# A denominator tile with a step of its own, larger packets, and a new order of issue in an attention and gated MLP kernel

## The chip, the cores and the metric

The kernel runs on one core of a Trainium2 chip. The metric is the device time of one execution in microseconds; lower is better. Engines are named as in the profile: PE (TensorE, matmuls), DVE (VectorE), ACT (ScalarE), POOL (GpSimd), SP (SyncE, which here issues the DMAs).

## The reference

Eight batches of 12 heads, 448 positions, head size 64. Attention with a soft cap on the scores is followed by a feed-forward part whose second half is mixed over the positions.

```python
scores = scale * np.matmul(q, k.transpose(0, 1, 3, 2))
scores = cap * np.tanh(scores / cap)
scores = scores - np.max(scores, axis=-1, keepdims=True)
attn = np.exp(scores)
attn = attn / (np.sum(attn, axis=-1, keepdims=True) + 1e-09)
x = np.matmul(attn, v)            # heads side by side: B, S, 768
...
h = np.maximum(x @ w_in, 0.0)
u, v = (h[..., :d_ff // 2], h[..., d_ff // 2:])
v_n = (v - mu) / np.sqrt(var + 1e-06)
v_s = np.einsum('ts,bsd->btd', w_spatial, v_n) + b_spatial[None, :, None]
return ((u * v_s) @ w_out).astype(np.float32)
```

## The kernel before

Work is cut into 24 quads (four heads of one batch, three quads a batch) and eight feed-forward parts. A quad in `quad_bnd` loads two raw tiles of q and k (`raw`) and four tiles of v, and makes seven groups of scores on PE (`sc`, four 64x64 matmuls in fp32). Each group is followed by a tanh on ACT, every two of them by one exponential (the last group has one of its own), and by a PE group that multiplies the exponentials with v into `x` (`pv`). Scores have two buffers, so group n can start when tanh n-2 is done.

The denominators take a side way. DVE folds the exponentials to their maximum and sum (`red`, `st`). For the first three quads PE makes the sums, with a matrix of ones (`ones`), and they go through DRAM (`td`) into the small tile `dt`. ACT shifts rows of `st` into `sh`, DVE combines both in `dt` and takes the reciprocal, two DMAs write it to DRAM (`rd`), and two DMAs broadcast it over the partitions (`rr`). Then DVE multiplies it into the copied `x` (`xf`), ACT and DVE make a high and a low half of it (`xg`), and the feed-forward part can use it: large matmuls of 128 rows, called `moe` here.

No engine's order is written out. `Plan.order` simulates the engines with fixed costs, and takes at each time the ready task with the lowest key; keys come from tables (`BND_KEY`, `BND_ADJ`) of about 130 numbers. The chosen order is recorded, and each engine then runs its instructions in that order, each as soon as its semaphores allow. SP issues all DMAs, in one order too. A task with an `allocs` list claims a buffer when it is taken. On PE a change from the 64-row matmuls to the large ones, or back, adds `STICK` to a key. The first weights are split into high and low parts (`w`, `wy`, `wi_h`, `wi_l`) during the first quads, on POOL, DVE and ACT.

Quads are counted from 0, and groups of scores and tanhs from 1, over the whole run.

Of the kernel before, what the change touches and what calls it, by code (L numbers as in the profile page):

```python
# [42 lines left out]
class Plan:  # L43
# [165 lines left out]
def gpc(n):  # L209
# [29 lines left out]
BND_KEY = dict(ld=15.1316, vld=10.6595, sc=-4.3972, th=0.8221, ex=-13.3346, pv=2.8747, sm=5.6221, mx=2.7207,  # L239
               dn=-3.5316, ev=-2.5342, x=1.255, moe=3.3159, span=11.7552, step=-1.2625, mv=-7.4324, vld_=0.4935, sc_=0.475,  # L240
               th_=0.213, ex_=2.8729, pv_=0.0973, sm_=0.5533, mx_=0.887)
BND_ADJ = dict(sc0=1.8257, sc1=1.698, sc2=0.6056, sc3=3.487, sc4=2.4891, sc5=0.9848, sc6=1.9465, sc7=1.2566,
               sc8=-0.2027, sc9=-0.0525, sc10=-1.0199, sc11=-1.6861, sc21=0.372, sc22=0.2759, sc23=-0.0304, mx0=4.147, mx1=2.3102,
               mx2=-1.5569, mx3=-2.5816, mx4=-1.7021, mx5=-3.8682, mx6=-3.7708, mx7=-2.1194, mx8=2.2658, mx9=6.0412, mx10=4.2055,
               mx11=1.3621, mx21=-0.5191, mx22=-1.2175, mx23=5.0057, sm0=1.8357, sm1=-4.3389, sm2=0.1127, sm3=-1.9888,
               sm4=-3.2252, sm5=-6.4566, sm6=-4.1062, sm7=-2.4598, sm8=-0.1718, sm9=4.6664, sm10=2.3463, sm11=0.4051,
               sm21=-1.2777, sm22=-3.1044, sm23=2.1372, dn0=-6.9641, dn1=1.8515, dn2=-0.9662, dn3=3.7809, dn4=8.6087, dn5=5.0673,
               dn6=1.1656, dn7=-2.366, dn8=0.4341, dn9=2.5001, dn10=4.9471, dn11=-4.3505, dn21=14.2648, dn22=10.8391, dn23=8.4438,
               x0=-1.2869, x1=-4.0561, x2=-5.6099, x3=-5.4773, x4=2.351, x5=0.6484, x6=4.0904, x7=0.1021, x8=2.4533, x9=6.1666,
               x10=4.3613, x11=1.3018, x21=-0.0656, x22=-3.6008, x23=0.1225, moe0=-0.4749, moe1=-0.3715, moe2=-0.6357,  # L250
               moe3=-0.003, moe7=-4.8205, span0=0.237, span1=0.5291, span2=-5.1693, span3=-3.6031, span7=51.1417, mv0=3.2517,
               mv1=1.1849, mv2=5.0071, mv3=5.7847, mv7=-5.1134, wi0=-11.8899, wi1=-7.682, wi2=-25.3033, wi3=9.6125, wi4=12.6292,
               wi5=4.2564, wi6=0.1225, wi7=-1.8938, wi8=-6.6204, wi9=0.3494, wi10=-1.8774, wi11=-9.6153, ws0=-12.9749, ws1=4.598,
               ws2=-15.4035, ws3=-9.2649, wo0=-5.5216, wo1=-4.7934, wo2=-5.3784, wo3=1.0364)
# [12 lines left out]
def attn_moe(ctx, tc, bounded, shared, qk, v, qk2, v2, cap, w_in, w_sp, w_out, out):  # L267
# [183 lines left out]

    def head_any(b, h, vt, vdep, xf, rr, after):
# [102 lines left out]
    def quad_bnd(b, n):  # L555
# [5 lines left out]
        for c in range(2):  # L561
            hp = 2 * n + c
            t = Buf("xg" if b * NP + hp in SPARE else "raw")
            raw.append(t)
# [12 lines left out]
        for i in range(NB):
# [22 lines left out]
            def pv(g=i // 2, tp=tp):  # L600
                for j in range(2 if g < 3 else 1):
                    for c in range(2):
                        for e in range(2):
# [1 line left out]
                            nc.tensor.matmul(x.t[e * D:(e + 1) * D, c, :S], lhsT=vts[g].t[c * D:(c + 1) * D, (2 * j + e) * D:(2 * j + e + 1) * D],  # L605
                                             rhs=tp.t[c * D:(c + 1) * D, j * PW + e * S:j * PW + (e + 1) * S], start=(k == 0), stop=(k == NB - 1))

            prev = add("T", FF * w // PW, kk("pv", i), pv, [ex, prev, tvs[i // 2]], [vts[i // 2], tp, x], [x] if i == 1 else [], name="pv", mode="R")
# [32 lines left out]
        d = add("V", 106, kk("dn"), lambda: nc.vector.tensor_tensor(sec(0), st.t[:96, :n1], sh.t[:96, :n1], op=ALU.max), d,  # L641
                [st, sh, dt], [dt], name="mred2")
        if by_pe:
# [300 lines left out]
```

## Time and profile before

| what | value |
|---|---|
| median of 3 runs | 734.66 us (734.47 to 735.39) |
| the profiled execution's own time | 735.29 us |
| its span, first to last instruction | 733.5 us |
| granted TensorE clock, mean | 0.994 of 2.4 GHz |
| DMA, mean over the span | 91 GB/s |

The span is what the trace covers; 1.8 us of the profiled execution lie around it. Busy times are shares of the span by engine. PE's busy time holds pipelined matmuls with modelled ends, so that 98% busy does not say that PE works at its peak.

### The profile page before, as it was taken

To read this page: it belongs to the slowest core of one execution; us is meant where nothing else is said; L and a number is where in the kernel's file an instruction comes from. 1 tells how busy PE (TensorE), PEld (TensorE's weight loads), DVE (VectorE), ACT (ScalarE), POOL (GpSimd) and SP (SyncE) were. 2 spreads that over 40 slices of the span, in tenths; PEclk is the share of its full clock that TensorE was granted. 3 is DMA by queue.
4 is the path that set the end of the run, shared out by engine and by line. 5 is a ranking of instruction groups with operands and counts; after the bars stand their busy time and mean duration, and the time that the engine had idled before them with its cause. 6 is when DMAs were issued, how large, how long until landed. Compare 5 with 4: busy or idle time off the path is not lost.

```text
span 733.5 us, 12340 instructions
## 1 busy us (share of the span) xinstructions
PE 716.0 (98%) x4902; PEld 485.3 (66%) x4902; DVE 609.6 (83%) x825; ACT 481.4 (66%) x648; POOL 79.0 (11%) x69
## 2 busy tenths in 40 slices
PE   8997999999999999999999999999999999999997
PEld 2333675574587586955778557767659576679896
DVE  4999999999999998949999299989899598884620
ACT  6999865858856957388573794867773865833421
POOL 1353011500100002000210003000020001000100
PEclk9998999999999999999999999999999999999999
DMA  7556232533212432052230431214311321002002
GB/s 268 192 192 200 67 111 63 164 102 107 90 32 85 143 100 76 1 150 82 72 102 11 140 103 33 69 44 160 101 47 56 101 76 51 26 26 88 14 2 80
DMA packets 43167, 66.52 MB, mean 91 GB/s; under 512 B 8782, under 2 KB 33884, under 8 KB 43100
## 3 DMA queue, kind: packets, MB, share of 16 engines
q1 hardware_dynamic: 43100, 65.64, 28.3%
q8 instruction: 40, 0.66, 0.4%
q14 instruction: 27, 0.22, 0.1%
HBM read 54.42 MB, written 11.20 MB: 89 GB/s over the span
## 4 chain that ended last, share of the span: by engine, by line
PE 63%; DVE 21%; ACT 6%; DMA 5%; issue 3%; SPq 1%; POOL 0%; DVEq 0%; ACTq 0%
PE ps_s L584 10%; PE ps_x L605 9%; DVE red L623 8%; PE ps_acc L859 4%; PE ps_acc L860 4%; PE ps_acc L861 4%; PE ps_acc L743 4%; PE ps_acc L744 4%; PE ps_acc L745 4%; DMA rr<-rd 3%; PE ps_acc L768 2%; PE ps_acc L770 2%; PE ps_acc L769 2%; ACT tp L595 2%; PE ps_acc L837 2%
## 5 line engine op out<-in xcount | busy, mean ns | idle before, releaser
L588 ACT ACTIVATE tp<-ps_s,capt 128x896 f32<-128x896 f32 x168 | 162.3, 1005 | 19.7 <-PE ps_s L584 13.7
L595 ACT ACTIVATE tp<-tp,capt 128x1792 f32<-128x1792 f32 x96 | 154.3, 1609 | 1.5
L623 DVE TENSOR_TENSOR red<-red,tp 128x1792 f32<-128x1792 f32 x90 | 140.0, 1555 | 14.7 <-ACT tp L595 13.2
L584 PE MATMUL ps_s<-raw 64*64 64x448 f32 x1344 | 147.1, 544 | 3.0 <-ACT tp L588 2.7
L605 PE MATMUL ps_x<-tp,v 64*64 64x448 f32 x1344 | 140.6, 537 | 2.0 <-ACT tp L595 1.7
L623 DVE TENSOR_TENSOR red<-tp 128x1792 f32<-128x1792 f32 x45 | 90.9, 2021 | 24.1 <-ACT tp L595 23.1
L605 PEld LDWEIGHTS ps_x<-tp,v 64*64 64x64 f32 x1344 | 50.4, 133 | 78.2 <-issue 67.8
L584 PEld LDWEIGHTS ps_s<-raw 64*64 64x64 f32 x1344 | 46.2, 132 | 80.4 <-issue 43.8
L792 POOL TENSOR_TENSOR lst<-lst,capt 128x1 f32<-128x1 f32 x32 | 38.6, 1208 | 521.8 <-DVE lst L790 521.8
L743 PE MATMUL ps_acc<-xg,wi_h 128*128 128x448 f32 x180 | 67.7, 376 | 3.2 <-ACT xg L345 3.2
L744 PE MATMUL ps_acc<-xg,wi_h 128*128 128x448 f32 x180 | 66.1, 367 | 1.2 <-DVE xg L341 1.2
L745 PE MATMUL ps_acc<-xg,wi_l 128*128 128x448 f32 x180 | 66.1, 367 | 0.0
L859 PE MATMUL ps_acc<-xg,wo_h 128*128 128x448 f32 x176 | 65.2, 371 | 0.4 <-DVE o L844 0.3
L860 PE MATMUL ps_acc<-xg,wo_h 128*128 128x448 f32 x176 | 64.0, 364 | 0.5 <-DVE xg L341 0.5
L861 PE MATMUL ps_acc<-xg,wo_l 128*128 128x448 f32 x176 | 63.6, 361 | 0.0
L690 DVE TENSOR_TENSOR xf<-xf,rr 128x448 f32<-128x448 f32 x48 | 44.4, 951 | 20.8 <-DMA rr<-rd 20.8
L345 ACT CAST xg<-o 128x448 fp32r<-128x448 f32 x32 | 17.9, 566 | 61.5 <-DVE o L844 53.5
L623 DVE TENSOR_TENSOR red<-red 128x896 f32<-128x896 f32 x45 | 50.6, 1123 | 0.5
L631 DVE STREAM_TRANSPOSE red<-red 128x896 f32<-128x896 f32 x45 | 49.6, 1103 | 0.5
L768 PE MATMUL ps_acc<-wi_h,xg 128*128 128x512 f32 x126 | 50.0, 397 | 0.0
L633 DVE TENSOR_REDUCE st<-red 128x28 f32<-128x896 f32 x45 | 48.6, 1079 | 0.8
L769 PE MATMUL ps_acc<-wi_l,xg 128*128 128x512 f32 x126 | 49.1, 390 | 0.0
(141 smaller groups left out, 1121.0 us busy)
## 6 DMA issues: line engine op xcount, KB each, us to landing
raw<-in_qk SPq DMA_DIRECT2D x48, 448.0 KB
rr<-rd SPq DMA_DIRECT2D x48, 224.0 KB
out<-o SPq DMA_DIRECT2D x48, 224.0 KB
v<-in_v SPq DMA_DIRECT2D x72, 128.0 KB
w<-in_w_in SPq DMA_DIRECT2D x12, 512.0 KB
xg<-in_w_out SPq DMA_DIRECT2D x12, 256.0 KB
v<-in_v SPq DMA_DIRECT2D x24, 64.0 KB
rd<-dt SPq DMA_DIRECT2D x48, 3.5 KB
```

Of the source, the lines that this page charges most:

```text
L584: nc.tensor.matmul(ps.t[c * D:(c + 1) * D, e, :S], lhsT=f(raw[c].t)[r, k:k + D], rhs=f(raw[c].t)[r, :S], start=True, stop=True)
L588: th = add("A", act(PW, 1), kk("th", i), lambda ps=ps, tp=tp, o=o: nc.scalar.activation(out=tp.t[:, o:o + PW].rearrange("p (e q) -> p e q" ...
L595: ex = add("A", act_s(w, 1), kk("ex", i), lambda tp=tp, w=w: nc.scalar.activation(out=tp.t[:, :w], in_=tp.t[:, :w], func=AF.Exp, scale=ca) ...
L605: nc.tensor.matmul(x.t[e * D:(e + 1) * D, c, :S], lhsT=vts[g].t[c * D:(c + 1) * D, (2 * j + e) * D:(2 * j + e + 1) * D], rhs=tp.t[c * D:(c ...
L623: nc.vector.tensor_tensor(o_(), i0(), i1(), op=op)
L743: nc.tensor.matmul(ps, lhsT=wi1_h[:, c, fs], rhs=x[:, XH:], start=(c == 0), stop=False)
L744: nc.tensor.matmul(ps, lhsT=wi1_h[:, c, fs], rhs=x[:, :S], start=False, stop=False)
L745: nc.tensor.matmul(ps, lhsT=wi1_l[:, c, fs], rhs=x[:, XH:], start=False, stop=(c == NP - 1))
L768: nc.tensor.matmul(ps, lhsT=x[:, XH:][:, ts], rhs=wi2_h[:, c], start=(c == 0), stop=False)
L859: nc.tensor.matmul(ps, lhsT=wo_h[:, c, ns], rhs=g[:, XH:], start=(c == 0), stop=False)
L860: nc.tensor.matmul(ps, lhsT=wo_h[:, c, ns], rhs=g[:, :S], start=False, stop=False)
L861: nc.tensor.matmul(ps, lhsT=wo_l[:, c, ns], rhs=g[:, XH:], start=False, stop=(c == 3))
```

## The change

The small tile `dt` is claimed by a task of no duration on SP (`room`), which waits for the first reduced column, in place of DVE's maximum; the two loads of the sums wait for `room` and no longer for the maximum. The reciprocals are laid out in DRAM so that one half of the partitions takes one run of 3584 bytes, in place of two runs of 1792. A quad's v is loaded in two pieces of up to 512 numbers a partition in place of four of up to 256, into two buffers in place of four. The planner's costs for DMAs and for a few DVE steps are new, and so are all numbers of the tables.

```diff
-    TURN, STICK = 180.0, 2.7208
+    TURN, STICK = 180.0, 3.6644
...
-                        took.lat = dma + 1000.0 - took.end
+                        took.lat = dma + 900.0 + 0.55 * took.lat - took.end
...
-HW, HH, XL, XF = 475, 650, 50, 4 / 360
+HW, HH, XL = 400, 620, 50
+def dm(packets, size):
+    return packets * (4.0 + 0.0016 * size)
...
-    "v": (4 * D, F32, 4), "tp": (2 * PW, F32, 6),
+    "v": (8 * D, F32, 2), "tp": (2 * PW, F32, 6),
...
-BND_KEY = dict(ld=15.1316, vld=10.6595, sc=-4.3972, th=0.8221, ex=-13.3346, pv=2.8747, sm=5.6221, mx=2.7207,
+BND_KEY = dict(ld=18.5712, vld=14.6317, sc=-4.6854, th=5.4736, ex=-9.6613, pv=2.9704, sm=6.41, mx=3.1479,
...
-        vts, tvs = [Buf("v") for _ in range(4)], []
-        for g in range(4):
-            w = min(4 * D, PW - 4 * D * g)
+        vts, tvs = [Buf("v") for _ in range(2)], []
+        for g in range(2):
+            w = min(8 * D, PW - 8 * D * g)
...
-            prev = add("T", FF * w // PW, kk("pv", i), pv, [ex, prev, tvs[i // 2]], [vts[i // 2], tp, x], [x] if i == 1 else [], name="pv", mode="R")
+            prev = add("T", FF * w // PW, kk("pv", i), pv, [ex, prev, tvs[i // 4]], [vts[i // 4], tp, x], [x] if i == 1 else [], name="pv", mode="R")
...
-        d = add("V", 106, kk("dn"), lambda: nc.vector.tensor_tensor(sec(0), st.t[:96, :n1], sh.t[:96, :n1], op=ALU.max), d,
-                [st, sh, dt], [dt], name="mred2")
+        room = add("S", 0, kk("dn"), lambda: None, [done[0]], [dt], [dt])
+        d = add("V", 106, kk("dn"), lambda: nc.vector.tensor_tensor(sec(0), st.t[:96, :n1], sh.t[:96, :n1], op=ALU.max), [*d, room],
+                [st, sh, dt], name="mred2")
...
-                in_=td.t[2 * c * S:2 * (c + 1) * S].rearrange("(e p b) -> p e b", e=2, b=QB)), [d, *outs], [td, dt], lat=XL) for c in range(2)]
+                in_=td.t[2 * c * S:2 * (c + 1) * S].rearrange("(e p b) -> p e b", e=2, b=QB)), [room, *outs], [td, dt],
+                lat=dm(64, 4 * QB)) for c in range(2)]
...
-            out=rd.t[2 * c * S:2 * (c + 1) * S].rearrange("(e p b) -> p e b", e=2, b=QB),
-            in_=dt.t[2 * c * 32:(2 * c + 1) * 32, :n1].rearrange("p (e b) -> p e b", b=QB)), [d], [dt, rd], [] if c else [rd], lat=XL)
-            for c in range(2)]
+            out=rd.t.rearrange("(e c p b) -> c p e b", e=2, c=2, b=QB)[c],
+            in_=dt.t[2 * c * 32:(2 * c + 1) * 32, :n1].rearrange("p (e b) -> p e b", b=QB)), [d], [dt, rd], [] if c else [rd],
+            lat=dm(64, 4 * QB)) for c in range(2)]
...
-            out=two(rr.t)[e * D:(e + 1) * D],
-            in_=rd.t.rearrange("(c e q) -> c e q", c=2, e=2)[:, e].unsqueeze(0).broadcast_to([D, 2, S])), d, [rd, rr],
-            [] if e else [rr], lat=XF * D * PW) for e in range(2)]
+            out=rr.t[e * D:(e + 1) * D], in_=rd.t.rearrange("(e q) -> e q", e=2)[e].unsqueeze(0).broadcast_to([D, PW])), d, [rd, rr],
+            [] if e else [rr], lat=dm(64, 4 * PW)) for e in range(2)]
```

What the new tables do shows in the rows of the engines. On PE, where quad 3's scores meet the first large matmuls of batch 0, the rows of before are these (`raw_157` and `raw_158` hold quad 3's heads; two rows with the same pair of tiles are one group of scores):

```order
L743 MATMUL ps_acc<-xg,wi_h 128x448
L744 MATMUL ps_acc<-xg,wi_h 128x448
L745 MATMUL ps_acc<-xg,wi_l 128x448
L584 MATMUL ps_s<-raw_157 64x448 x2
L584 MATMUL ps_s<-raw_158 64x448 x2
L584 MATMUL ps_s<-raw_157 64x448 x2
L584 MATMUL ps_s<-raw_158 64x448 x2
L743 MATMUL ps_acc<-xg,wi_h 128x448
```

Two groups, the 27th and 28th, stand between the first six large matmuls and the next 18. The same place now (lines have moved by 7 or 8; `raw_60` and `raw_61` hold quad 4's heads):

```order
L751 MATMUL ps_acc<-xg,wi_h 128x448
L752 MATMUL ps_acc<-xg,wi_h 128x448
L753 MATMUL ps_acc<-xg,wi_l 128x448
L591 MATMUL ps_s<-raw_157 64x448 x2
L591 MATMUL ps_s<-raw_158 64x448 x2
L591 MATMUL ps_s<-raw_157 64x448 x2
L591 MATMUL ps_s<-raw_158 64x448 x2
L591 MATMUL ps_s<-raw_60 64x448 x2
L591 MATMUL ps_s<-raw_61 64x448 x2
L591 MATMUL ps_s<-raw_60 64x448 x2
L591 MATMUL ps_s<-raw_61 64x448 x2
L751 MATMUL ps_acc<-xg,wi_h 128x448
```

Four groups, the 27th to the 30th, stand there. On ACT at the same place, before, from the tanh of group 24 (`ACTIVATE tp<-ps_s` is a tanh, `ACTIVATE tp<-tp` an exponential, `CAST xg<-xf` the copies of x):

```order
L588 ACTIVATE tp<-ps_s,capt 128x896
L660 COPY u<-ps_acc 128x14x32 x2
L588 ACTIVATE tp<-ps_s,capt 128x896 x2
L345 CAST wi_h<-wy 128x512
L595 ACTIVATE tp<-tp,capt 128x1792
L345 CAST xg<-xf 128x448 x2
L345 CAST xg<-xf 128x64 x2
L345 CAST xg<-xf 128x448
L639 COPY sh_164<-st 32x28
L345 CAST xg<-xf 128x64
L639 COPY sh_164<-st 32x28
L588 ACTIVATE tp<-ps_s,capt 128x896
```

The last row is tanh 27. Now, from tanh 23 and 24:

```order
L595 ACTIVATE tp<-ps_s,capt 128x896 x2
L602 ACTIVATE tp<-tp,capt 128x1792
L668 COPY u<-ps_acc 128x14x32 x2
L595 ACTIVATE tp<-ps_s,capt 128x896
L352 CAST wi_h<-wy 128x512
L602 ACTIVATE tp<-tp,capt 128x1792
L595 ACTIVATE tp<-ps_s,capt 128x896 x2
L602 ACTIVATE tp<-tp,capt 128x1792
L352 CAST xg<-xf 128x448 x2
L352 CAST xg<-xf 128x64 x2
L352 CAST xg<-xf 128x448
```

Tanh 25, 26 and 27 and the three exponentials now stand ahead of the copies of x; the second tanh pair of this piece is 26 and 27, and tanh 28 follows behind the copies and shifts.

## Rows read from the trace of the kernel before

**Rows 1.** The page, parts 1 and 3: busy time by engine; DMA queue.

```profile
PE 716.0 (98%) x4902; PEld 485.3 (66%) x4902; DVE 609.6 (83%) x825; ACT 481.4 (66%) x648; POOL 79.0 (11%) x69
...
q1 hardware_dynamic: 43100, 65.64, 28.3%
```

**Rows 2.** Table of stages: window, length, busy by engine, clock, DMA share, GB/s.

```profile
6.20:63.46 57.26, 53.50 (x544) 20.30 (x544) 49.78 (x67) 53.98 (x59) 21.97 (x19) 1.00 0.65 217
63.46:69.60 6.14, 3.39 (x26) 1.39 (x22) 5.18 (x6) 5.20 (x7) 2.69 (x2) 1.00 0.90 246
69.60:76.40 6.80, 5.21 (x13) 4.33 (x14) 6.80 (x13) 6.68 (x12) 0.95 (x1) 0.50 0.32 107
...
87.50:653.00 565.50, 562.48 (x3838) 384.24 (x3834) 504.16 (x669) 380.72 (x511) 50.36 (x40) 1.00 0.26 82
```

**Rows 3.** Timeline of PE, 62 to 72 us: start, length, what; idle before it.

```profile
62.55 0.98 PE L584 MATMUL ps_s<-raw 64*64 64x448 f32 x8 [0.24 <-ACT tp L588]
63.46 0.47 PE L743 MATMUL ps_acc<-xg,wi_h 128*128 128x448 f32 x1
63.77 0.36 PE L744 MATMUL ps_acc<-xg,wi_h 128*128 128x448 f32 x1
63.98 0.37 PE L745 MATMUL ps_acc<-xg,wi_l 128*128 128x448 f32 x1
...
65.00 1.85 PE L584 MATMUL ps_s<-raw 64*64 64x448 f32 x16
70.03 0.74 PE L743 MATMUL ps_acc<-xg,wi_h 128*128 128x448 f32 x1 [3.18 <-ACT xg L345]
71.93 0.74 PE L744 MATMUL ps_acc<-xg,wi_h 128*128 128x448 f32 x1 [1.16 <-DVE xg L341]
```

**Rows 4.** Timeline of PE, 77 to 88 us, two changes of kind.

```profile
77.33 0.36 PE L745 MATMUL ps_acc<-xg,wi_l 128*128 128x448 f32 x1
77.62 1.74 PE L584 MATMUL ps_s<-raw 64*64 64x448 f32 x16
79.17 1.68 PE L605 MATMUL ps_x<-tp,v 64*64 64x448 f32 x16
...
85.18 2.44 PE L605 MATMUL ps_x<-tp,v 64*64 64x448 f32 x24
87.55 0.47 PE L743 MATMUL ps_acc<-xg,wi_h 128*128 128x448 f32 x1
```

**Rows 5.** Timeline of ACT, 59 to 80 us.

```profile
59.29 1.79 ACT L595 ACTIVATE tp<-tp,capt 128x1792 f32<-128x1792 f32 x1
60.99 0.60 ACT L345 CAST wi_h<-wy 128x512 fp32r<-128x512 f32 x1
61.49 1.00 ACT L588 ACTIVATE tp<-ps_s,capt 128x896 f32<-128x896 f32 x1
...
63.93 1.88 ACT L588 ACTIVATE tp<-ps_s,capt 128x896 f32<-128x896 f32 x2
...
68.95 1.79 ACT L345 CAST xg<-xf 128x448 fp32r<-128x448 f32 x5 [0.94 <-DVE xf L690]
...
71.49 1.01 ACT L588 ACTIVATE tp<-ps_s,capt 128x896 f32<-128x896 f32 x1
...
78.69 1.90 ACT L588 ACTIVATE tp<-ps_s,capt 128x896 f32<-128x896 f32 x2 [1.22 <-PE ps_s L584]
```

**Rows 6.** The chain that ended last, 60 to 90 us: start, length, what.

```profile
62.82 5.15 DMA rr<-rd
...
67.99 1.77 DVE xf L690 x2
```

**Rows 7.** What SP's queue waited for: total us, times, longest us.

```profile
SPq L573 <- PE ps_x L605: 204.4, 77, 16.2
```

**Rows 8.** Timeline, 314 to 327 us, DVE and PE.

```profile
322.79 1.79 DVE L690 TENSOR_TENSOR xf<-xf,rr 128x448 f32<-128x448 f32 x2 [8.90 <-DMA rr<-rd]
325.28 0.98 PE L584 MATMUL ps_s<-raw 64*64 64x448 f32 x8 [0.72 <-ACT tp L588]
```

More of the change, by code (lines that the diff above doesn't have):

```diff
@@ L238 @@
 ANY_W_KEYS = 2, 0.5, 8, 9, 1, 5, 0.5
-BND_KEY = dict(ld=15.1316, vld=10.6595, sc=-4.3972, th=0.8221, ex=-13.3346, pv=2.8747, sm=5.6221, mx=2.7207,
[L240 to L254, printed above, removed]
@@ new lines @@
+BND_KEY = dict(ld=18.5712, vld=14.6317, sc=-4.6854, th=5.4736, ex=-9.6613, pv=2.9704, sm=6.41, mx=3.1479,
+               dn=-1.4871, ev=-2.6224, x=1.0342, moe=3.0315, span=11.4953, step=-1.3582, mv=-7.7287, vld_=0.524, sc_=0.1428,
+               th_=0.0225, ex_=2.6161, pv_=0.0477, sm_=0.8136, mx_=0.8166)
+BND_ADJ = dict(sc0=4.4511, sc1=1.2269, sc2=0.263, sc3=3.8403, sc4=2.7496, sc5=2.0076, sc6=1.2149, sc7=0.0243,
+               sc8=-1.3055, sc9=1.8269, sc10=-0.0885, sc11=-3.0459, sc21=0.2319, sc22=0.2568, sc23=-1.6178, mx0=4.301, mx1=3.4181,
+               mx2=2.7815, mx3=-0.9955, mx4=-4.8134, mx5=-2.1667, mx6=-3.358, mx7=-1.6784, mx8=-0.9705, mx9=-1.8315, mx10=4.1645,
+               mx11=3.5442, mx21=0.5504, mx22=-1.5649, mx23=0.5323, sm0=-0.143, sm1=-15.8015, sm2=-5.867, sm3=-4.0789,
+               sm4=-7.8128, sm5=-4.1115, sm6=-6.3291, sm7=-3.6173, sm8=-2.6664, sm9=1.7341, sm10=3.2093, sm11=0.5576,
+               sm21=-1.6192, sm22=0.4821, sm23=2.0578, dn0=-2.0769, dn1=-1.1287, dn2=0.5808, dn3=3.2267, dn4=4.0345, dn5=1.9565,
+               dn6=5.9263, dn7=6.4464, dn8=2.1056, dn9=1.9402, dn10=-2.0468, dn11=-1.9079, dn21=13.0834, dn22=-5.7844,
+               dn23=15.6871, x0=-3.1346, x1=-5.2468, x2=-4.9133, x3=-3.6007, x4=1.7024, x5=0.2015, x6=1.9404, x7=0.5166,
+               x8=4.4152, x9=2.5249, x10=0.2325, x11=-1.2873, x21=0.0722, x22=1.5031, x23=1.1572, moe0=-1.4528, moe1=0.6266,
+               moe2=-1.1431, moe3=-2.6968, moe7=6.2237, span0=2.4365, span1=-3.7305, span2=-5.1287, span3=-1.7337, span7=44.7627,
+               mv0=1.4655, mv1=0.9689, mv2=7.2222, mv3=5.107, mv7=1.3427, wi0=-9.1384, wi1=-7.1511, wi2=-33.3265, wi3=12.1226,
+               wi4=11.1369, wi5=9.3981, wi6=-3.3322, wi7=2.7702, wi8=-23.0305, wi9=0.402, wi10=-2.8499, wi11=-8.3206,
+               ws0=-13.3077, ws1=-0.1981, ws2=-18.9279, ws3=-13.4915, wo0=-2.3063, wo1=-0.3664, wo2=2.2653, wo3=5.628)
@@ L255 @@
 BND_V_FIRST = 1
 WARM, WARM_N = 14, 512
-BND_W_KEYS = -2.6025, -2.3988, 2.613, 12.9605, -0.7052, 10.7987, 1.6426
+BND_W_KEYS = -4.9927, -1.031, 1.0682, 10.1588, -1.4103, 10.2989, 1.2718
 SPARE = ()
@@ L368, in split_f32 @@
         hi, lo = ws_h[:, c, :], ws_l[:, c, :]
-        a = add("S", HW, key, lambda: load(t.t[:n, :S], rows), allocs=[t], lat=XF * n * S)
+        a = add("S", HW, key, lambda: load(t.t[:n, :S], rows), allocs=[t], lat=dm(n, 4 * S))
         if c == 3:
-            a = add("S", HW, key, lambda: load(t.t[n:, :S], rows), [a], [t], lat=XF * n * S)
+            a = add("S", HW, key, lambda: load(t.t[n:, :S], rows), [a], [t], lat=dm(n, 4 * S))
         b = add("V", dve2(S), key, lambda: nc.vector.tensor_copy(hi, t.t[:, :S]), [a], [t])
@@ L460, in ld @@
             nc.sync.dma_start(out=raw.t[D:128], in_=qk[b, h, :, :raw_n])
-        t0 = add("S", 2 * HW, k - 2.0, ld, allocs=[raw], lat=XF * 128 * 896)
+        t0 = add("S", 2 * HW, k - 2.0, ld, allocs=[raw], lat=dm(128, 3584))
         t1 = add(E_HI, ct(E_HI, 896), k - 1.2, lambda: copy(E_HI, hi.t, raw.t), [t0], [raw], [hi])
@@ L604, in pv @@
                             k = 2 * g + j
[L605 removed]
+                            nc.tensor.matmul(x.t[e * D:(e + 1) * D, c, :S], lhsT=vts[g // 2].t[c * D:(c + 1) * D, (4 * (g % 2) + 2 * j + e) * D:(4 * (g % 2) + 2 * j + e + 1) * D],
                                              rhs=tp.t[c * D:(c + 1) * D, j * PW + e * S:j * PW + (e + 1) * S], start=(k == 0), stop=(k == NB - 1))
[L608 removed]
+            prev = add("T", FF * w // PW, kk("pv", i), pv, [ex, prev, tvs[i // 4]], [vts[i // 4], tp, x], [x] if i == 1 else [], name="pv", mode="R")
         xf, rr = Buf("xf"), Buf("rr")
```

16 lines of the change are left out of this document (8 added, 8 removed).

## The prediction

> **What bounds the kernel now.** I read the page first: TensorE (PE) is counted busy for 716.0 us of a span of 733.5 [rows 1], so the order of work on PE sets the end, and only time in which PE does no useful work can be won. The table of stages then says where that time lies [rows 2]. From 87.5 to 653 us PE is idle for 565.50 - 562.48 = 3.0 us. Up to 63.46 it is idle for 57.26 - 53.50 = 3.8 us, and in the two short stages after that for 2.75 and 1.59 us. In the second of these the granted clock is 0.50, that is 1.2 GHz in place of 2.4.
>
> The timeline of PE shows what it waits for there [rows 3]. A group of scores (four 64x64 matmuls, two records each, so 8 records) starts at 62.55, just after the 24th tanh ends on ScalarE (ACT) at 61.49 + 1.00 [rows 5]: with two buffers of scores, group n waits for tanh n-2. Six matmuls of the second half follow at 63.46, two score groups at 65.00, and then PE waits 3.18 us for ACT's copies of x tiles, and 1.16 us for the low part that VectorE (DVE) makes. The clock falls 2.75 us after PE went idle (66.85 to 69.60) and comes back 6.8 us later. The chain that ended last names the cause [rows 6]: the broadcast of the reciprocals lands 5.15 us after its second issue, and DVE's multiplication starts at 67.99. I price this stage as follows. A group costs 0.751 us: from 79.17 to 85.18 lie four pieces of two groups [rows 4]; a large matmul costs 0.20 [rows 3]. From 6.2, where PE has ended its warm-up, to 87.55 it does 83 groups and 24 large matmuls, 62.4 + 4.8 = 67.2 us, in 81.3 us. So 14 us are lost in the opening, and that is the part that a new order can move.
>
> **The change part by part.** *Broadcasts.* Two broadcasts of 64 packets of 3584 bytes replace two of 128 packets of 1792; the bytes are the same. The hardware queue moved 43,100 packets in 28.3% of 16 engines' span [rows 1], 0.283 x 16 x 733.5 / 43,100 = 77 ns for a mean packet of 1523 bytes. If time went by packets alone, the half of 256 packets would save 128 x 77 / 16 = 0.6 us of each pair; if by bytes, nothing. It is on the chain in three quads of the opening. Between 0 and -1.8 I take the end near bytes, since the pair's landing of 5.15 us is many times the 0.6: **-0.3 us**.
>
> The Trainium skill, "DMA: Bandwidth & Descriptors", section "Anatomy of one DMA — SWDGE (gpsimd) path", has about 2.0 us fixed and the rest by bytes at 436 GB/s, mostly for the confirmation at the end. By it, as an estimate, 448 KB take 2.0 + 1.05 = 3.05 us with either packet size, and this term would be 0; the trace has 5.15, with a weight load and a v load asked for just ahead, so its size is not confirmed here.
>
> *Two v loads for four.* SP's issues fall from 96 to 48, and SP does not bound. But a buffer now holds half a quad, and is free only when two pv steps in place of one have read it. Before, SP waited 204.4 us in total (77 times) with a v load for such a buffer [rows 7], and everything behind it in SP's queue waited too. PE reads the first half of a quad's v many groups after the half was freed in the opening too (counted in the new order: over ten groups, 7.5 us), and a landing like that of [rows 6] is 5.15. I take 0, with the price of a late half below.
>
> *Denominators' tile.* The load of the sums no longer waits for the 106-element maximum but for the tile alone. SP has a raw load or a v load ahead of it in both orders, so 0; the upper bound of a gain is below the 0.3 of the first term.
>
> *The order, opening.* Counted on ACT's order, ahead of tanh 24 stand nine 1792-wide exponentials in place of ten; the other kinds are equal in number. One costs 1.70 us from its start to the next one's [rows 5]. So the first 68 groups end 1.7 us earlier, at 61.8, if ACT is as full as before. The exponential follows at once, and tanh 25 starts at 63.93 as before. From there the order is another one: a weight copy (0.50), an exponential (1.70), tanh 26 and 27 (1.90), an exponential (1.70), and only then the x copies and shifts, at 70.6 us, where the tiles of 67.99 have long been multiplied: ACT's wait of 0.94 before them is gone. They take 68.95 to 71.49 = 2.54, tanh 28 about 1.0, so it ends at 74.1. PE now has four score groups, not two, ahead of its 18 large matmuls, and the fourth needs tanh 28. So the 18 begin at 75.1 and not at 70.03. At the full clock they take 3.6 + 0.2 and end at 78.9; before they ended at 77.62, and two groups (1.5 us) are done in addition: 1.3 - 1.5 = -0.2. At the low clock, by the same lags as in [rows 2, 3], the low stretch reaches from about 72.7 (2.75 after PE idles at 69.9) to 79.5: twelve of the 18 take 0.37, they end at 80.9, and the net is +1.8. PE has gaps from 63.3 on in the new order, so the low stretch can also lie earlier and be over; between -0.2 and +1.8 I take **+0.5 us**. ACT, for its part, no longer idles 1.22 us at 78.69 for group 29, which now stands before the 18; that is the cover that keeps the rest of the opening level.
>
> *The order, changes of kind.* PE changes between groups and large matmuls 62 times before and 68 times now, counted in its rows. Going to the large ones costs 87.55 - 85.18 - 3 x 0.751 = 0.12 and 0.31 - 0.21 = 0.10 in the next step; going back costs 0.29 - 0.20 = 0.09, and the first piece of two groups is 1.74 and not 1.68 long [rows 3, 4]. A pair costs 0.37, a change 0.18: 6 x 0.18 = **+1.1 us**. No other work hides it, since PE itself stands still.
>
> *The order, later.* At 322.79 DVE has waited 8.90 us for a broadcast, because two reciprocals stand side by side with almost no DVE work behind them; ACT stuck behind it, and PE lost 0.72 us at 325.28 [rows 8]. In the new order the eleventh and twelfth reciprocal are far apart, and the two pairs that now stand side by side have four or more folds' worth of work behind them. I take **-0.7 us**; bounds are -3.0 (all PE idleness of that stage) and 0.
>
> Sum: -0.3 + 0.5 + 1.1 - 0.7 = +0.6 us. Against the profiled execution (735.29, of which 733.5 is its span) that is 735.9; its median of three is 734.66, so the forecast is 734.66 + 0.6 = **735.3 us**, no change that a measurement of this kernel can tell: about 0.2%, or 1.5 us, is what it can tell from none, 733.2 to 736.1.
>
> **Rivals.** *Faster: the clock stays up.* If PE's shorter pauses keep 2.4 GHz, the opening gives -0.2; if also ACT loses its small waits for weight copies, another microsecond; and if the other late waits go, -3.0. With +1.1 for the changes of kind: -0.2 - 1.0 - 3.0 + 1.1 = -3.1, 731.6 us. For it: every loss of [rows 2] is a wait on an order, and all of it was set anew. Against it: the 18 matmuls are moved behind a later tanh.
>
> *Slower: the low clock holds through all 18.* Then they take 18 x 0.37 = 6.7 us and end at 82.0 (75.1 + 6.7 + 0.2), ACT waits for group 31 behind them, and the net is 82.0 - 77.6 - 1.5 = +2.9. With nothing won on broadcasts or later: +2.9 + 1.1 = +4.0, 738.7 us. It decides from the point at which tanh 28 ends later than 74. The rows speak for it in that 3.18 us of waiting was enough before.
>
> *Slower too: v halves come late.* A half that is freed one pv step later lands one step later; if PE waits a pair of groups (1.5 us) in two quads of the opening, +3.0 + 0.6, 738.3 us. Against it is the distance of ten groups.
>
> **How the numbers follow.** The forecast has 0.38, with its own range from 733.0 to 737.0; the faster rival 0.34, the low clock 0.20, the late halves 0.08. The range takes in the two main rivals' times and a little beyond, 730.8 to 738.8, since the bounds of the later stage are the widest. Of the forecast's 0.38 I put 0.03 below 733.2, 0.06 above 736.1. So faster 0.37, the same 0.29, slower 0.34.
>
> **What would show it.** In the changed kernel's profile: the first six large matmuls near 62 and not 63.46; four score groups and then a pause before the 18, which start near 75; a stretch at clock 0.50 that ends within them; ACT without a wait of 1.2 us behind them; the third quad's x copies near 86 as before; after that changes of kind of 0.18, now more of them. The broadcast lands 0 to 0.6 us sooner. A DVE wait of 9 us no longer stands in the list of waits. I am wrong if the opening loses clearly less or more than 14 us, or if between 87 and 653 PE's idle time is far from 3 us: the order there was compared only at a few places.

## The result, and the profile after

The changed kernel takes 745.07 us (742.6 to 745.37, 4 executions), the kernel before 734.57 beside it: a ratio of 1.0137, 95% interval 1.0122 to 1.0152. That is 10.5 us slower, and above the predicted range of 730.8 to 738.8. The profiled execution took 744.95 us, with a span of 743.2.

The page's busy times and DMA queue, which answer to [rows 1]:

```profile
PE 721.6 (97%) x4902; PEld 490.0 (66%) x4902; DVE 611.4 (82%) x825; ACT 481.0 (65%) x648; POOL 64.2 (9%) x69
...
q1 hardware_dynamic: 33116, 65.64, 27.6%
```

The queue carries the same bytes in 33,116 packets instead of 43,100. DVE and ACT are as busy as before, within 0.3%. The span grew by 9.7 us, PE's counted busy time by 5.6; the count of matmuls is the same, and those at the low clock take longer (end of this section).

Table of stages (window, length, busy of PE, PE's weight loads, DVE, ACT and POOL, clock, DMA share, GB/s), as in [rows 2]. The first stage ends with the first 68 groups of 64x64 matmuls (scores, products with v, and the sums by the matrix of ones), the third with the 18 large matmuls:

```profile
7.05:66.20 59.15, 55.28 (x544) 24.59 (x544) 51.04 (x68) 54.39 (x59) 22.31 (x19) 0.97 0.64 213
66.20:78.40 12.20, 6.00 (x43) 1.99 (x39) 11.55 (x16) 12.07 (x19) 2.52 (x3) 0.85 0.46 150
78.40:83.70 5.30, 5.30 (x26) 4.53 (x22) 4.59 (x9) 4.08 (x4) 0.00 (x0) 0.70 0.29 88
...
87.50:653.00 565.50, 560.39 (x3813) 382.10 (x3806) 503.31 (x666) 381.64 (x513) 36.93 (x40) 1.00 0.27 83
```

In the last row PE is idle for 565.50 - 560.39 = 5.1 us, in the same window of [rows 2] for 3.0.

Timeline of PE, the places where it waits and where the stages begin:

```profile
1.17 5.79 PE L907 MATMUL wps<-warm 128*128 128x512 bf16 x14 [1.17 <-DVE capt L910]
7.07 1.73 PE L591 MATMUL ps_s<-raw 64*64 64x448 f32 x16
...
53.08 2.16 PE L612 MATMUL ps_x<-tp,v 64*64 64x448 f32 x16 [1.72 <-ACT tp L602]
...
66.21 0.47 PE L751 MATMUL ps_acc<-xg,wi_h 128*128 128x448 f32 x1
...
70.52 1.88 PE L591 MATMUL ps_s<-raw 64*64 64x448 f32 x16 [1.91 <-ACT tp L595]
76.69 1.77 PE L591 MATMUL ps_s<-raw 64*64 64x448 f32 x8 [4.29 <-ACT tp L595]
78.39 0.74 PE L751 MATMUL ps_acc<-xg,wi_h 128*128 128x448 f32 x1
...
83.68 1.74 PE L591 MATMUL ps_s<-raw 64*64 64x448 f32 x16
...
257.07 0.50 PE L776 MATMUL ps_acc<-wi_h,xg 128*128 128x512 f32 x1 [1.40 <-ACT o L352]
...
339.61 0.47 PE L867 MATMUL ps_acc<-xg,wo_h 128*128 128x448 f32 x1 [1.92 <-ACT o L352]
```

These starts split the 9.7 us, since PE does the same work in both kernels:

| stretch on PE | before | after | more |
|---|---|---|---|
| start of the first group, behind the warm-up | 6.22 | 7.07 | 0.85 |
| first 68 groups | 63.46 - 6.22 = 57.24 | 66.21 - 7.07 = 59.14 | 1.90 |
| 24 large matmuls and four groups (before: two, plus 1.50 for two more) | 77.62 - 63.46 + 1.50 = 15.66 | 83.68 - 66.21 = 17.47 | 1.81 |
| all the rest of the span | 733.5 - 77.62 - 1.50 = 654.4 | 743.2 - 83.68 = 659.5 | 5.1 |

So in this profile the opening lost 3.7 us, the rest 5.1, and 0.85 stands ahead of any work that was changed.

**The opening.** Timeline of ACT at the two places that PE waits for:

```profile
50.77 0.56 ACT L352 CAST xg<-xf 128x448 fp32r<-128x448 f32 x1 [0.99 <-DVE xf L698]
51.25 1.78 ACT L602 ACTIVATE tp<-tp,capt 128x1792 f32<-128x1792 f32 x1
...
73.09 1.77 ACT L352 CAST xg<-xf 128x448 fp32r<-128x448 f32 x5
...
75.63 1.91 ACT L595 ACTIVATE tp<-ps_s,capt 128x896 f32<-128x896 f32 x2
```

At 50.77 ACT copies the first tile of x; that copy waits for DVE, and DVE for the first broadcast. The tenth exponential stands behind it, and PE waits 1.72 us for it. At 73.09 five copies of x, then a sixth and two shifts, stand ahead of tanh 28 (the first of the two in the row at 75.63), and PE waits 4.29 us for that tanh with the fourth of its four groups, ahead of the 18.

**The rest.** Timeline of SP around the wait of 1.92 us at 339.61, then that of ACT there:

```profile
329.45 1.09 SPq L689 DMA_DIRECT2D rr<-rd  x2
330.59 0.58 SPq L580 DMA_DIRECT2D v<-in_v  x1
331.26 0.85 SPq L573 DMA_DIRECT2D raw<-in_qk  x2
332.48 8.02 SPq L873 DMA_DIRECT2D out<-o  x4
```

```profile
331.91 0.54 ACT L352 COPY o<-ps_acc 128x448 f32<-128x448 f32 x1
...
333.23 0.55 ACT L352 COPY o<-ps_acc 128x448 f32<-128x448 f32 x1
...
339.02 1.12 ACT L352 COPY o<-ps_acc 128x448 f32<-128x448 f32 x2 [4.30 <-DMA out<-o]
```

Two broadcasts, a half of v and two raw loads are issued just ahead of the first store of a result. There are two tiles for results (`o`), so ACT's third copy waits 4.30 us until the first store has landed, and PE waits for the bank of PSUM that this copy empties. The chain of work that ended last shows the store, and one of the broadcasts of the opening:

```profile
44.82 4.35 DMA rr<-rd
...
332.48 6.47 DMA out<-o
```

The page's list of DMA issues has the median landing of a store at its end:

```profile
out<-o SPq DMA_DIRECT2D x48, 224.0 KB, 2.1
```

That is 2.1 us, over the seven of the 48 stores whose landing the trace has; this one took 6.47. Near 257 the same happens behind four broadcasts, issued in one row from 248.59. Three lines of the lists of waits sum it up: ACT's waits for stores before and after (total us, times, longest us), and DVE's for broadcasts after:

```profile
ACT o L345 <- DMA out<-o: 0.6, 1, 0.6
```

```profile
ACT o L352 <- DMA out<-o: 15.7, 5, 4.3
```

```profile
DVE xf L698 <- DMA rr<-rd: 3.9, 5, 1.3
```

ACT's waits for stores grew from 0.6 to 15.7 us. DVE's waits for broadcasts, among them the 8.90 us of [rows 8], fell from 20.8 us in all to 3.9.

Last, the table of windows at the stretches in which the clock was 1.2 GHz, ahead of the end of the kernel:

```profile
54.25:57.65 3.40, 3.40 (x24) 1.33 (x20) 3.40 (x8) 3.26 (x5) 0.00 (x0) 0.50 0.54 175
74.75:81.55 6.80, 4.86 (x17) 3.12 (x18) 6.09 (x14) 6.67 (x11) 0.00 (x0) 0.50 0.10 29
341.00:344.40 3.40, 3.40 (x11) 3.02 (x10) 1.77 (x1) 0.00 (x0) 0.00 (x0) 0.50 0.20 73
```

Before there was one, of 6.8 us [rows 2]; now there are three. The two new ones begin 1.2 and 1.4 us after PE resumed from waits of 1.72 and 1.92 us, and each is filled with work: by the clock alone, 3.4 us at half of it are 1.7 us lost. The second can be checked against e9 below, the same kernel without that stretch: from the matmul that ended the wait to the one that starts at 344.92 here, PE took 5.31 us, in e9 3.72, so it cost 1.6.

### The profile page after: what moved, and what is told of

Read it like the earlier page. It is cut to its first block, busy times and chain, and to the rows that moved or that the text cites. A ratio compares the mean times of both kernels' runs of the same rounds, so it can differ in the third digit from the quotient of the medians.

```text
span 743.2 us, 12233 instructions
## 1 busy us (share of the span) xinstructions
PE 721.6 (97%) x4902; PEld 490.0 (66%) x4902; DVE 611.4 (82%) x825; ACT 481.0 (65%) x648; POOL 64.2 (9%) x69
## 2 busy tenths in 40 slices
DMA packets 33182, 66.51 MB, mean 89 GB/s; under 512 B 8014, under 2 KB 17756, under 8 KB 33116
## 3 DMA queue, kind: packets, MB, share of 16 engines
q1 hardware_dynamic: 33116, 65.64, 27.6%
## 4 chain that ended last, share of the span: by engine, by line
PE 67%; ACT 14%; DVE 13%; DMA 3%; issue 2%; SPq 1%; DVEq 0%; ACTq 0%
PE ps_s L591 10%; PE ps_x L612 9%; ACT tp L595 6%; ACT tp L602 5%; DVE red L630 5%; PE ps_acc L751 4%; PE ps_acc L753 4%; PE ps_acc L752 4%; PE ps_acc L867 4%; PE ps_acc L868 4%; PE ps_acc L869 3%; PE ps_acc L776 3%; PE ps_acc L778 3%; PE ps_acc L777 3%; PE ps_acc L845 2%
## 5 line engine op out<-in xcount | busy, mean ns | idle before, releaser
L591 PE MATMUL ps_s<-raw 64*64 64x448 f32 x1344 | 151.7, 548 | 7.4 <-ACT tp L595 7.1
L612 PE MATMUL ps_x<-tp,v 64*64 64x448 f32 x1344 | 142.1, 539 | 2.7 <-ACT tp L602 2.7
L591 PEld LDWEIGHTS ps_s<-raw 64*64 64x64 f32 x1344 | 48.3, 133 | 83.8 <-issue 41.6
L800 POOL TENSOR_TENSOR lst<-lst,capt 128x1 f32<-128x1 f32 x32 | 29.1, 911 | 542.5 <-DVE lst L798 454.5
L776 PE MATMUL ps_acc<-wi_h,xg 128*128 128x512 f32 x126 | 50.4, 400 | 1.4 <-ACT o L352 1.4
L778 PE MATMUL ps_acc<-wi_h,xg 128*128 128x512 f32 x126 | 49.2, 390 | 0.0
L630 DVE TENSOR_TENSOR red<-red 128x896 f32<-128x896 f32 x45 | 48.8, 1085 | 0.4
```

The source lines that it names most:

```text
L591: nc.tensor.matmul(ps.t[c * D:(c + 1) * D, e, :S], lhsT=f(raw[c].t)[r, k:k + D], rhs=f(raw[c].t)[r, :S], start=True, stop=True)
L612: nc.tensor.matmul(x.t[e * D:(e + 1) * D, c, :S], lhsT=vts[g // 2].t[c * D:(c + 1) * D, (4 * (g % 2) + 2 * j + e) * D:(4 * (g % 2) + 2 * j ...
L630: nc.vector.tensor_tensor(o_(), i0(), i1(), op=op)
L776: nc.tensor.matmul(ps, lhsT=x[:, XH:][:, ts], rhs=wi2_h[:, c], start=(c == 0), stop=False)
```

## Experiments

The theory: the time was lost by the order of issue, at a few places, and not by the new DMAs. Rivals: halves of v that come free later; a loss spread over the whole order; a limit of ACT that no swap moves. All runs were timed in five rounds, those of one group beside the kernel before on the same chip.

| run | us | ratio to before, 95% |
|---|---|---|
| e1, new DMAs in the old order | 736.13 | 1.0010 (0.9998 to 1.0022) |
| e2, old DMAs in the new order | 743.79 | 1.0126 (1.0099 to 1.0152) |
| e3, exponential ahead of the copy | 741.91 | 1.0108 (1.0080 to 1.0136) |
| e4, two raw loads exchanged | 743.06 | 1.0116 (1.0097 to 1.0135) |
| e5, stores first | 740.26 | 1.0082 (1.0065 to 1.0098) |
| e6, e3 and tanh ahead of the copies | 742.14 | 1.0098 (1.0080 to 1.0117) |
| e7, e5 and e6 together | 739.87 | 1.0067 (1.0049 to 1.0084) |
| e8, before, broadcast first | 733.59 | 0.9990 (0.9980 to 1.0001) |
| e9, changed kernel again | 742.24 | 1.0108 (1.0088 to 1.0129) |
| e10, e7 without the moved broadcast | 737.80 | 1.0048 (1.0030 to 1.0065) |
| e11, e8 and a low part moved | 733.89 | 0.9997 (0.9986 to 1.0008) |

Groups on one chip: e1 to e4, e5 to e8, e9 to e11, with 735.35, 734.80 and 734.06 us for the kernel before. Where two of these intervals overlap, the times alone do not tell the runs apart, as with e3, e4, e5 and e9. So each run's profile is split at the same starts on PE as above (us; in the rows with the old order, the two groups that stand elsewhere are allowed for with 1.50, as above):

| profile | first group starts | first 68 groups | 24 large matmuls and four groups | all the rest |
|---|---|---|---|---|
| before | 6.22 | 57.24 | 15.66 | 654.4 |
| e1, old order | 6.81 | 56.83 | 16.25 | 654.5 |
| changed kernel | 7.07 | 59.14 | 17.47 | 659.5 |
| e9, the same again | 6.90 | 59.06 | 17.41 | 657.5 |
| e2, new order | 6.21 | 59.47 | 16.80 | 657.6 |
| e4, new order but for one exchange | 6.18 | 59.32 | 16.77 | 657.6 |
| e3 | 6.00 | 57.44 | 17.94 | 657.5 |
| e6 | 7.32 | 57.24 | 16.06 | 659.9 |
| e5 | 5.83 | 58.26 | 17.12 | 655.7 |
| e7 | 5.97 | 57.64 | 16.84 | 656.5 |
| e10 | 7.28 | 57.31 | 15.94 | 654.7 |

With the new order of stores, the rest is 3.1 to 3.2 us longer than before in four profiles, and 5.1 and 5.5 in the two in which the clock fell near 340 (the changed kernel and e6).

**e1 and e2: the DMAs and the order apart.** The planner's result is replaced by a recorded list, so that each engine issues in the other kernel's order:

```diff
+    issue = [plan.tasks[i] for i in ORDER] if bounded else plan.order()
...
-        for t in plan.order():
+        for t in issue:
```

> The changed kernel's DMAs (two v loads of half a quad, broadcasts of 64 packets of 3584 bytes, tile of denominators claimed on its own), issued in the order that the kernel before had on every engine; where that order had two quarter loads of v, the half stands at the place of the second. Theory 'order': the 10 us are lost by the new order of issue, so this run takes 733.5 to 736, a ratio of 0.999 to 1.002 to the kernel before. Theory 'halves': the v halves, which come free later and hold up SP's queue and the stores and broadcasts behind them, cost the time; then it takes 739 to 745, and SP's waits for v are longer than 204 us in total. Theory 'packets' (larger packets land sooner): 732 to 733.5.

> The kernel before with its four v loads and its 128 packets of 1792 bytes, but issued in the changed kernel's order on every engine; two quarter loads of v stand at the place of a half. Theory 'order': 743 to 746, with PE's waits of 1.7 us near 53, 1.9 and 4.3 us near 70 and 77, and about 1.9 us near 340 all there. Theory 'halves': 734 to 739, and the wait near 340 is gone because the v loads stand less long in SP's queue.

The new DMAs in the old order cost 0.1% or nothing (736.13 us is 0.13 above the range of the theory 'order', the ratio inside it); the old DMAs in the new order cost 1.26%, nearly all of the 1.37. This decides it: the order lost the time. In e1, the waits of SP's queue for v and two broadcasts on the chain:

```profile
SPq L694 <- PE ps_x L726: 186.5, 35, 18.6
```

```profile
46.59 3.98 DMA rr<-rd
62.79 5.56 DMA rr<-rd
```

SP waits less for halves than it did for quarters, 186.5 us against 204.4 [rows 7]. The broadcasts land after 3.98 and 5.56 us, those of 1,792-byte packets at the same places after 4.05 (on the chain of before at 46.34) and 5.15 [rows 6]. So neither 'halves' nor 'packets' holds. From PE's list of waits in e2:

```profile
PE ps_acc L883 <- ACT o L460: 1.7, 1, 1.7
```

```profile
PE ps_acc L974 <- ACT o L460: 0.6, 1, 0.6
```

The 1.7 us are the wait near 257 (it ends at 256.27); the one near 340 is 0.6 us only, not the 1.9 that the theory 'order' had. The waits of 2.2 and 4.3 us in the opening stand. So the order carries the time, but how long PE waits behind stores differs from one execution to the next.

**e3: one swap on ACT.** A helper takes the n-th task of a name out of the list and puts it ahead of (with a last 1: behind) the m-th of another:

```diff
+        move("exp", 10, "xh", 1)
```

> The changed kernel with one swap on ACT: the tenth exponential, which stood behind the first copy of x (and so behind the first broadcast), is issued ahead of that copy. Theory 'one place in the order starts it': PE's wait of 1.72 us at 53.08 goes, the clock does not fall at 54.3, the first 68 groups end 2.5 to 3.4 us sooner, and the run takes 741.5 to 743. Rival 'ACT is the limit there anyway': ACT does the same work up to the 24th tanh, the clock alone is won or not even that, and the run takes 744 to 745.5.

Timeline of PE in e3:

```profile
50.48 1.73 PE L612 MATMUL ps_x<-tp,v 64*64 64x448 f32 x16
...
63.44 0.47 PE L751 MATMUL ps_acc<-xg,wi_h 128*128 128x448 f32 x1 [0.68 <-ACT u L668]
...
74.30 1.77 PE L591 MATMUL ps_s<-raw 64*64 64x448 f32 x8 [3.57 <-ACT tp L595]
```

The wait of 1.72 us is gone, the clock did not fall there, and the 68 groups took 63.44 - 6.00 = 57.44 us, the 57.24 of before within 0.2, against 58.3 to 59.5 in the five profiles with the exponential behind the copy. The time of 741.91 is in the range, but its interval overlaps that of e4, so the profile is the evidence here. The end of this stage now waits 0.68 us for ACT's copies of the sums (`u`): the swap won back what was lost, and not the 1.7 us that I had predicted on top.

**e4: a miss that became a control.**

```diff
+        move("raw", 27, "out", 18, 1)
+        move("raw", 28, "raw", 27, 1)
```

> The changed kernel with one move on SP: two raw loads of 448 KB, issued at 331.3 just ahead of six stores of results, are issued behind these six. Theory 'the stores wait behind the raw loads in the queue': the first store lands 2 to 3 us after its issue instead of 6.5, ACT's wait of 4.3 us at 339 and PE's of 1.92 at 339.6 go, and so does the stretch at half clock behind it (3.4 us, a cost of 1.7): 741 to 742.5. Rival 'it is the two tiles for results, not the queue': the stall stays at 1 us or more and the run takes 744 to 745.5.

The second line put the first load back, since the numbers shift with the first move: the two raw loads only changed places with each other, ahead of the stores as before. The run says nothing on stores. It is the changed order but for that exchange, at 743.06.

**e5: stores first.** The move of e4 done rightly, and one more near 249:

```diff
+        move("raw", 28, "out", 18, 1)
+        move("raw", 27, "out", 18, 1)
+        move("rr", 18, "out", 10, 1)
+        move("rr", 17, "out", 10, 1)
```

> The changed kernel with two places of SP's order mended: the two raw loads ahead of six stores near 331 now stand behind these stores, and of four broadcasts ahead of three stores near 249 the last two now stand behind the first of these. Theory 'stores behind large transfers hold up ACT, then PE': ACT's waits for stores (15.7 us in five waits) fall below 8, PE's wait of 1.4 us near 257 and of 1.2 to 1.9 near 340 both fall below 0.6, and the run takes 1.5 to 3.5 us less than the 743 to 745 of the changed kernel: 739.5 to 743. Rival 'PE is late there for another reason': the same waits stay, 743 to 745.

SP's timeline in e5, where six stores now stand together and the raw loads follow at 340.95, and ACT's line of waits:

```profile
329.74 11.11 SPq L873 DMA_DIRECT2D out<-o  x6
```

```profile
ACT o L352 <- DMA out<-o: 10.0, 4, 3.4
```

PE's waits at both places are gone, and near 340 the clock stays up; the rest of the span is 655.7 us, against 657.5 to 659.9 with the raw loads ahead of the stores. The time of 740.26 is in the range, though its interval overlaps those of the changed order (e4, e9). ACT's waits for stores fell only to 10.0, not below 8; behind those that are left PE does not wait for ACT's copies of results.

**e6: tanh 28 ahead of the copies as well.**

```diff
+        move("exp", 10, "xh", 1)
+        move("tanh", 28, "xh", 2)
```

> The changed kernel with two swaps on ACT: the tenth exponential ahead of the first copy of x, as before, and also the 28th tanh ahead of the next five copies and two shifts of quads 1 and 0, behind which it stood. Theory 'the 18 large matmuls wait for group 30, and that for tanh 28': PE's second wait of 3.6 to 4.3 us falls below 2.5, and the 18 start 1 to 2 us sooner against the first 68 groups than the 11 to 12 us that lay between; the run takes 739 to 741.5. Rival 'the copies are as late as the tanh': group 30 comes sooner, but the 18 start no sooner, since the copies come 1 us later; the run takes what the first swap alone took, 741.5 to 743.

Timeline of PE in e6:

```profile
64.56 0.48 PE L751 MATMUL ps_acc<-xg,wi_h 128*128 128x448 f32 x1 [0.69 <-ACT u L668]
...
72.87 0.98 PE L591 MATMUL ps_s<-raw 64*64 64x448 f32 x8 [1.73 <-ACT tp L595]
73.79 0.47 PE L751 MATMUL ps_acc<-xg,wi_h 128*128 128x448 f32 x1
75.64 0.74 PE L752 MATMUL ps_acc<-xg,wi_h 128*128 128x448 f32 x1 [1.38 <-DVE xg L348]
...
80.62 1.74 PE L591 MATMUL ps_s<-raw 64*64 64x448 f32 x16
```

The wait for tanh 28 fell from 4.29 to 1.73, and 1.38 came in its place for the low part of x, because the copies are later. From the first large matmul to the end of the 18 it is 80.62 - 64.56 = 16.06 us, against 17.47 of the changed kernel and 15.66 of before. Both swaps together bring the opening to within 0.4 us of before, so both mechanisms are right, by the profile. The run's time of 742.14 does not show it: it is above its range and inside the rival's, and in the profiled execution the place near 337 was worse, a wait of 2.2 us and a stretch at half clock.

**e7 and e10: all together, and without the moved broadcast.** e7 has the edits of e5 and e6, e10 leaves out the two lines with "rr".

> The changed kernel with the two swaps on ACT and the two moves on SP together. Theory 'a few places in the order make the loss': the gains add up, 736.5 to 739.5; what is left against the kernel before are the six more changes of kind, 1.1 us, and small waits. Rival 'the loss is spread over the order': 740 to 743.

> The changed kernel with the two swaps on ACT and the raw loads behind the stores, but the four broadcasts near 249 left where they were. Theory 'the moved broadcast made a new wait': PE's wait of 1.6 us for a tanh at 258, which the run with all moves showed, is gone, that of 0.9 to 1.4 behind the stores near 255 is back, and the run takes what all moves took, 738.5 to 741. Rival 'the moved broadcast was a gain': 741 to 743.

e7 took 739.87, just above its range. Its profile has a new wait: the broadcast moved behind a store came late, ACT's copies of x waited 2.96 us at 254.70 for DVE's product with it, and PE for a tanh behind them:

```profile
258.45 1.88 PE L591 MATMUL ps_s<-raw 64*64 64x448 f32 x16 [1.63 <-ACT tp L595]
```

In e5, with the same move, PE's wait there is only 0.18 us, so the move makes this wait possible and not sure. e10 has no wait there, and 737.80 us, less than either theory had it; the theory's wait behind the stores near 255 did not come back as 0.9 to 1.4 but as 0.3. From ACT's and PE's lists of waits in e10:

```profile
ACT o L352 <- DMA out<-o: 6.9, 3, 2.8
```

```profile
PE ps_acc L776 <- ACT o L352: 0.3, 1, 0.3
```

Four tasks moved on ACT and SP (one exponential, one tanh, two raw loads) took 4.4 us off the 742.24 of e9 on the same chip, and here the intervals lie apart. By the stages of the profile, e10 is within 0.1, 0.3 and 0.3 us of before. So it wins back 2.8 of the 3.1 us that the rest loses in e9. Half of that lies where the raw loads were moved: the matmuls that run from 329.9 to 344.9 in the changed kernel, 15.0 us, take 12.6 in e9 and 11.2 in e10 and e5. The move is thus worth 1.4 us there, and 3.8 against an execution with the clock stretch; the other 1.4 of the 2.8 are spread over the rest of the span, and no edit of e10 explains them.

**e9: the changed kernel again.**

> The changed kernel once more, beside the kernel before on the same chip. Theory 'the time hangs on how often the clock falls': the same kernel shows times from 741.5 to 745.5, the longer ones at a mean granted clock of 0.990 and less, the shorter ones at 0.993 and more; the profile shows two to three stretches at half clock ahead of the end. Rival 'the places differ by chip': all times within 1 us of each other.

The executions lie between 741.06 and 744.86; the longest has a mean granted clock of 0.989, the others 0.992 to 0.995. The four of the first measurement had 0.988 to 0.990 and up to 745.37. Within 0.992 to 0.995 the order of the times does not follow the clock, so the theory holds for the long ones only. Beside the kernel before, the changed kernel is 8.2 us slower here and was 10.5 in the first measurement: the granted clock was lower then. In e9's profile the place near 339 reads, in PE's list of waits and in the table of windows:

```profile
PE ps_acc L867 <- ACT o L352: 1.1, 1, 1.1
```

```profile
339.00:345.00 6.00, 6.00 (x30) 5.41 (x29) 5.87 (x7) 2.80 (x8) 0.00 (x0) 1.00 0.33 122
```

A wait of 1.1 us in place of 1.92, and the clock stayed at 2.4 GHz. That place is the main difference between the two profiles' rests, 657.5 and 659.5 us.

**e8 and e11: is there more in the old order?** In the kernel before, the second quad's broadcasts go ahead of a weight load and a v load; e11 also moves a weight's low part on DVE behind the low parts of x:

```diff
+        move("rr", 3, "w", 11)
+        move("rr", 4, "w", 11)
+        move("w64", 56, "xl", 4, 1)
```

(The last line in e11 alone.)

> The kernel before with one move on SP: the second quad's two broadcasts, which stood behind a weight load of 512 KB and a v load of 128 KB, are issued ahead of these. Theory 'the broadcast waits for bytes ahead of it in the queue': it lands 1 to 2 us after sooner than at 68.0, the copies of x follow, PE's wait of 3.2 us at 70 falls to 1.5 to 2.5, and the run takes 0.5 to 2.5 us less than the kernel before, 732.5 to 734.5. Rival 'ACT is full there': ACT takes the exponential and the copies in turn and the 18 large matmuls start no sooner, or the weights come late instead: 734.5 to 737.

> The kernel before with its second quad's broadcasts issued ahead of a weight load and a v load, and on DVE the low part of a weight moved behind the three low parts of x tiles that the first 18 large matmuls wait for. Theory: PE's wait for DVE's low part falls from 1.2 to 1.4 us to 0.6 to 0.8, and with the earlier broadcast the run takes 732 to 734 against 735 of the kernel before. Rival 'the clock takes it back': the stretch at half clock covers what is won, 734 to 735.5.

Timeline of PE in e8, then in e11:

```profile
69.84 0.47 PE L743 MATMUL ps_acc<-xg,wi_h 128*128 128x448 f32 x1 [2.15 <-ACT xg L345]
```

```profile
70.84 0.47 PE L744 MATMUL ps_acc<-xg,wi_h 128*128 128x448 f32 x1 [0.84 <-DVE xg L341]
...
81.53 1.88 PE L584 MATMUL ps_s<-raw 64*64 64x448 f32 x16 [0.23 <-ACT tp L588]
```

The wait of 3.18 us of [rows 3] fell to 2.15, and in e11 the one for the low part to 0.84, with no stretch at half clock left in the opening. Yet the ratios are 0.9990 and 0.9997, and both intervals include 1. In e11 part of it is given back a little later: the 13 groups of [rows 4], 9.9 us in the kernel before, take 11.1, with a new wait at 81.53, which the old order had not, and one at 86.31. No version beat the kernel before beyond doubt.

## Why the prediction was wrong, step by step

- **Broadcasts, -0.3: no gain.** e1 has the larger packets and is not faster, 1.0010 with a lower end of 0.9998; its two landings are 0.07 us shorter and 0.41 us longer. So the end "by bytes" of that term fits. The Trainium skill, "DMA: Bandwidth & Descriptors", section "Anatomy of one DMA — SWDGE (gpsimd) path", has time go by bytes above a fixed part, which makes this term 0; e1 agrees with that form. Its 3.05 us are for one DMA alone on the gpsimd path, and these pairs, on SP's queue with others ahead, took 3.98 to 5.56.
- **Two loads of v, tile of denominators, 0: right within e1's interval.** e1 has them together with the larger packets, at -0.1 to +1.6 us, and SP waits less for v there; so the rival of late halves falls. What each of the three does alone was not run.
- **Opening, +0.5 (at most +1.8): it lost 3.7, and the step that failed is its first one.** "The first 68 groups end 1.7 us earlier, if ACT is as full as before": I had counted ACT's work ahead of tanh 24, and not looked at which row in it waits. The tenth exponential stood behind a copy that needs a broadcast; the groups took 1.9 us longer instead, 3.6 us off the forecast, with a clock stretch behind the wait. e3 shows the cause. The second step, the 18 large matmuls behind tanh 28, was right in kind and in size: from the end of the 68 groups (61.8) to the end of the 18 the forecast has 17.1 to 19.1 us, 17.8 at the value taken, and it took 17.47, with a wait of 3.57 (e3) to 4.29 us for that tanh. e6 shows it. The 18 began at 78.39 and not at 75.1, because all before them was late.
- **Changes of kind, +1.1: counted, not tested.** PE changes 68 times, as the order said, and a piece of two groups after large matmuls still takes 1.74 us (the row at 83.68; [rows 4]). No run changed their number alone. e10 keeps all 68 changes, and its stages behind the first start add up to only 0.7 us more than before, so the term is not seen by itself.
- **Later, -0.7 (between -3.0 and 0): the other step that failed.** The rest lost 5.1 us with the changes of kind in the first profile, 3.1 in e9's, so about +4.0 and +2.0 without the 1.1. The reason I gave was true: DVE's waits for broadcasts fell. But only 0.72 us of them had been PE's [rows 8]. What I did not look at is what stands behind such transfers in SP's order: result stores. At two places these hold up ACT and then PE, 1.40 us, and 1.92 us with 1.6 for the clock, 4.9 in all in the first profile. e5 and e10 show the stores: with the raw loads behind them the rest is 655.7 and 654.7 us, the latter 0.3 above before. The place near 340 alone is 3.8 us of that against the first profile, 1.4 against e9's; what remains of the loss in e9's profile is spread and not traced.
- **The rivals and the signs.** "Clock stays up" and "late halves" did not come. "Low clock through all 18" is nearest in kind, but the clock was low through about half of the 18 only, and that was not the main loss. Both signs of being wrong came: the opening lost 3.7 us more than its 14, and from 87.5 to 653 us PE is idle for 5.1 us, not 3. The bounds of the range came from the places that I had compared; "the order there was compared only at a few places" was the warning, and the range did not carry it.

What stays open: e10 is still 3.7 us above the kernel before by the medians (737.80 against 734.06), while the two profiles differ by 1.75, of which 1.06 is the later start of the first group and 0.7 lies behind it. No run tells where the other 2 us of the medians are lost. Why the clock falls in some executions and not in others of the same kernel is open too.

## What to carry to other kernels

When an order of issue is made anew, counting the work ahead of a point gives only a bound: look for each row that waits for something late (a broadcast, a load, another engine), and read what now stands behind it on the same engine. Do so on the queue that issues DMAs too: a small store behind large loads is a late store, and with two result tiles it stops the engine that empties PSUM. A wait that you see removed is worth what it cost the bounding engine, and not its own length.

## What the runs showed of the hardware that I had not expected

- In the changed kernel, waits of PE of 1.72 and 1.92 us were followed by stretches of 3.4 us at 1.2 GHz (54.25 and 341.00). At the second place a wait of 1.1 us was followed by none (e9). The length of the wait alone does not settle it: at the first place in e5 PE waited 1.82 us at 52.55, and the clock was 1.00 from 53 to 68 us. So a short wait can cost nearly twice its length, and the same kernel differs by 3.8 us between executions (741.06 to 744.86 in e9).
- The 14 warm-up matmuls, the same instructions started at 1.17 or 1.18 us in every profile, took from 4.55 us (e5) to 6.04 (e6). The 5.79 of the changed kernel and the 4.94 of the kernel before lie within that spread, so the 0.85 us between their first groups is not shown to come from the change.
- The landing of one store of 224 KB varied from 2.1 us in the median to 6.47, the long one behind two broadcasts, a half of v and two raw loads. With the raw loads behind the stores (e5), ACT no longer waited for a store there.
